# GpSimd's instructions in a hand-scheduled attention and convolution kernel: with and without semaphore ties to VectorE's planned instructions

## The chip, the core and the metric

The kernel runs on one core of a Trainium2 chip. The core has five engines with an instruction stream each: TensorE (PE in the profile; PEld is its weight load), ScalarE (ACT), VectorE (DVE), GpSimd (POOL) and SyncE (SP), which issues most of the DMAs. They meet only through semaphores. The metric is the device time of one execution in microseconds, lower is better.

## What is computed

From `q`, `k`, `v` and `x` (2048 positions, width 640) the kernel computes a gated sum of two branches:

```python
g = sigmoid((A_q * gate_w).sum(-1, keepdims=True))
a = A_q * (causal_long_convolution(kv, ssm_k) + kv * ssm_D)   # kv = short_convolution(A_k, 4 taps) * A_v
b = attention(B_x)   # the reference hands it x = A_q; 32 heads of 20, one shared key and value head
return g * a + (1 - g) * b
```

The attention has 32 heads x 2048 x 2048 scores, and each needs an exponential. The long convolution (over 2048 positions for each of 640 channels) is done through a discrete Fourier transform, written as matrix products with tables of cosines and sines.

## The kernel before

**The streams.** The kernel is a Python program that first collects every instruction as an `Op` (engine, function, operations it depends on, planned cost), then lets a planner, class `Scheduler`, run through planned time and fix the order of each engine's instructions, and then emits each engine's list with semaphore waits. Nothing is decided on the chip: each engine runs its list in order, and an instruction starts when its semaphores are there.

**Attention.** Scores of 128 keys x 512 queries are made by TensorE (line 1323) in PSUM, three or two tiles at a time. ScalarE takes the exponential of 1536 or 1024 columns at a time (line 1360, tiles `ETA` and `ETB`), and TensorE multiplies the result with the values (line 1413). This goes on from about 19 us to the end of the span. A part of the score tiles, named in the table `DVE_J`, has its exponential computed on VectorE: TensorE writes 128 x 512 scores in one of the banks 5 and 7, VectorE brings them to SBUF scaled (line 1393, `dW`, two of them), and three instructions on 128 x 1024 elements make a polynomial of them: lines 1405 and 1406 (`dX`) and 1408 (`ETd`). The last of these feeds TensorE's product again. There are 113 such exponentials. They read both operands from SBUF. Where the program marks an instruction of VectorE `port=True`, the planner takes it that it and a GpSimd instruction can't run at the same time; lines 1405, 1406 and 1408 are marked so, and the evacuations from PSUM are not.

**Normalising.** When a group of four heads is done, VectorE copies its sums (line 1487, `acc`), the reciprocals of the denominators go out to DRAM and come back broadcast (`rbc`), and GpSimd multiplies (line 1499), which for 24 of the 31 groups a DMA of SyncE stores.

**The convolution** fills what the attention leaves free. TensorE transforms the data and the filter (line 1705), VectorE brings the spectra to SBUF (line 1718 `X`, 1724 and 1726 `K`, in three buffers), and GpSimd multiplies them: six instructions per block (line 1738: three products `Pp<-X,K`, one sum `Pp<-Pp`, two `AB<-Pp`), 240 in all. TensorE transforms back from `AB` (line 1773). GpSimd also makes half of the tables (lines 998, 1008, 1010) earlier on. `Pp` has one buffer.

**The planner and GpSimd.** At each step the planner takes the engine whose planned time is least. For GpSimd, once the attention has started (`main_started`), `pool_may` says whether it may start now: not when VectorE is about to begin a marked instruction, yes when VectorE is in an unmarked one that still has some time to go, or when VectorE has nothing marked to do, or when the instruction has waited too long (`WAITP`, 6 us). `place` then fixes the instruction: it works out start and end, appends it to its engine's list, and, in the lines that the change touches, adds a dependency of a GpSimd instruction on a VectorE instruction. I call this a tie. `emit` turns each dependency that isn't covered by an earlier wait into a semaphore wait. The ties come after the start and end are worked out, so that the planner's order doesn't depend on them.

Of the kernel before, what the change touches and what calls it, by code (L numbers as in the profile page):

```python
# [40 lines left out]
HOLD = 0.05  # L41
# [130 lines left out]
class Scheduler:  # L172
# [305 lines left out]
    def place(self, op, e):  # L478
        t = self.t[e]
        op.eng = e  # L480
        if e == "pe":
            mode = MODE.get(op.name, "f")
            if mode != self.mode:
                t += SWITCH
                self.mode = mode
        if op.alts:
            for x in op.alts:
                self.cand[x].discard(op)
            op.fn, op.cost = op.alts[e]
        else:  # L490
            self.cand[e].discard(op)
        if op.main and e == "pe":
            for b in op.banks or ():
                if not self.bank_claimed[b]:
                    self.bank_claimed[b] = True
                    op.deps.update(self.bank_last[b])
        start = max(t, op.ready)
        if e == "pe" and start < COLD:
            op.cost *= 1.85
        if op.kind == "d":  # L500
            if op.nbytes:
                begin = max(start + 0.1, self.dma_bw)
                self.dma_bw = begin + op.nbytes / 300e3
                op.end = max(self.dma_bw, start + op.iss) + op.lat
            else:
                op.end = start + op.iss + op.lat
            self.t[e] = start + op.iss
            best = min(range(NLANES), key=lambda l: self.lanes[l][-1].end if self.lanes[l] else -1.0)
            op.lane = best
            if self.lanes[best]:  # L510
                op.deps.add(self.lanes[best][-1])
            self.lanes[best].append(op)
            op.value = 16 * len(self.lanes[best])
        else:
            if op.port and e == "dve":
                op.end = max(start, self.pool_until - PORTP) + op.cost
                self.port_until = op.end
            elif e == "pool":
                op.end = max(start, self.port_until - PORTD) + op.cost
                self.pool_until = op.end  # L520
            else:
                op.end = start + op.cost
            self.t[e] = op.end
        op.start = start
        op.placed = True
        if e == "pe" and op.cost > 0.05:
            self.active.append((op.end - op.cost * 0.92, op.end))
        if e == "pe":
            if op.name != "qk":
                self.rows = set()  # L530
            elif op.cont:
                self.rows.add(op.row)
            else:
                self.rows = {op.row}
        if op.name in ("tp0", "tp1"):
            b = STAGES[int(op.name[2])][2]
            self.bank_claimed[b] = self.bank_busy[b] = False
            self.bank_last[b] = [op]
            self.bank_ready[b] = op.end + LATX
        if op.name == "pv":  # L540
            if op.stage is not None:
                self.filler = self.filler2[op.stage]
            self.can_fill = not op.last
            self.acc = None
        elif op.name == "acc":
            self.acc = op
        if e == "pool" and self.main_started and HOLD:
            d = self.order["dve"]
            if len(d) > 1 and d[-1].end > t and not d[-1].port:
                op.deps.add(d[-2])  # L550
            elif len(d) > 1 and op.ready + TIED < t:
                op.deps.add(d[-1] if d[-1].end <= t else d[-2])
        self.order[e].append(op)
        self.linear.append(op)
        gr = op.grp
        if gr is not None:
            if e == "pe" and op in gr.mms:
                gr.pos += 1
                if gr.pos == len(gr.mms) and self.open is gr:
                    self.open = None  # L560
            elif op in gr.evacs:
                if all(x.placed for x in gr.evacs):
                    b = gr.bank
                    self.bank_busy[b] = False
                    self.bank_last[b] = [gr.mms[-1]] + list(gr.evacs)
                    self.bank_ready[b] = max(x.end + (LATX if self.main_started else LATS[x.eng, "pe"]) for x in gr.evacs)
        for s in op.succ:
            s.nun -= 1
            lat = 0.0 if (s.eng == "pe" and e == "pe") else self.lat_of(op, e, s.eng)
            s.ready = max(s.ready, op.end + lat)  # L570
            sg = s.grp
            if sg is not None and s.eng == "pe" and not (op.grp is sg):
                sg.nun -= 1
                sg.ready = max(sg.ready, op.end + lat)
                if sg.nun == 0:
                    self.gcand.add(sg)
            if s.nun == 0:
                self.enable(s)
# [91 lines left out]
PORTD = 0.14  # L670
PORTW = 0.2
COVER = 0.3
TIED = 0.1
COLD = 5.6
BUBBLE = 0.04
INB = ()
# [1242 lines left out]
```

## Time and profile before

| what | value |
|---|---|
| time, median of 3 runs | 856.3 us (855.84 to 857.56) |
| the profiled execution's own time | 857.9 us |
| its span, first to last instruction | 856.1 us |
| mean granted clock of TensorE | 0.996 |
| GpSimd busy in the span | 403.2 us, 357 instructions |
| VectorE busy in the span | 772.8 us, 984 instructions |
| line 1738, `Pp<-X,K`, 120 instructions: mean of one, idle time before them | 1388 ns, 114.2 us |
| line 1738, `AB<-Pp`, 80 instructions | 828 ns, 81.4 us |
| line 1738, `Pp<-Pp`, 40 instructions | 1343 ns, 55.3 us |
| lines 1405, 1406, 1408, 113 instructions each: mean of one | 1338, 1385, 1390 ns |
| line 1393, 226 instructions: mean of one | 683 ns |

How to read it: "busy" is the time in which an engine had an instruction in progress. "Idle before" is the time in which the engine stood still ahead of an instruction; the profile puts it down to the semaphore that came last, and names the instruction that gave it. An instruction that has started may still be held up inside; then its record is longer, and it counts as busy. A row of the timeline has the start in us from the span's start, the duration, engine, line, operation, tiles and shape, and in brackets the idle time ahead and what ended it.

### The profile page before, as it was taken

What the parts mean: (1) busy time and instruction counts of PE and PEld (TensorE: products, weight loads), DVE (VectorE), ACT (ScalarE), POOL (GpSimd) and SP (SyncE); (2) the same over time, 40 slices, a digit from 0 to 9 for tenths busy, and PEclk for the clock granted to TensorE, in tenths of its full rate; (3) what the DMA queues carried; (4) which work ended last, traced back from release to release, by engine and by line L of the source; (5) the groups of instructions that cost most, each with busy time, mean ns of one, the idle gap of its engine ahead of it and who ended that gap; (6) DMA issues with size and microseconds to landing.
All of it is one profiled execution on the core that took longest, in us unless ns stands there. A gap on an engine that the chain in (4) does not pass through costs nothing.

```text
span 856.1 us, 18905 instructions
## 1 busy us (share of the span) xinstructions
PE 833.9 (97%) x8094; PEld 349.3 (41%) x8105; DVE 772.8 (90%) x984; ACT 838.3 (98%) x750; POOL 403.2 (47%) x357
## 2 busy tenths in 40 slices
PE   9999999999999999999999999999999999999997
PEld 5244433443444434444334444444443443433334
DVE  7788989895998999999999999999988799989996
ACT  7999989999999999999999999999999999999997
POOL 3578403458464365446417664655666645000000
PEclk9999999999999999999999999999999999999999
DMA  6840240002110001000110202001000000411101
GB/s 190 204 113 15 38 82 21 15 13 65 37 43 20 15 20 28 25 21 21 39 47 20 45 20 46 26 10 43 20 20 16 20 8 8 113 38 60 40 31 44
DMA packets 55765, 36.31 MB, mean 42 GB/s; under 512 B 33057, under 2 KB 51714, under 8 KB 55682
## 3 DMA queue, kind: packets, MB, share of 16 engines
q1 hardware_dynamic: 55106, 34.90, 15.3%
q8 instruction: 63, 1.03, 0.5%
q10 hardware_dynamic: 576, 0.22, 0.1%
q14 instruction: 20, 0.16, 0.1%
HBM read 20.31 MB, written 8.51 MB: 34 GB/s over the span
## 4 chain that ended last, share of the span: by engine, by line
ACT 76%; PE 13%; DVE 8%; DMA 1%; issue 1%; SPq 0%
ACT ETA L1360 46%; ACT ETB L1360 31%; PE ps L1323 4%; PE ps L1413 3%; DVE dX L1406 2%; DVE dX L1405 2%; PE ps L1773 2%; DVE ETd L1408 1%; DVE dW L1393 1%; PE ps L1803 1%; PE ps L1705 1%; DMA xn<-in_A_q_dram 1%; PE ps L1859 1%; PE ps L1230 1%; DMA den<-acc 1%
## 5 line engine op out<-in xcount | busy, mean ns | idle before, releaser
L1360 ACT ACTIVATE ETA<-ps 128x1536 bf16<-128x1536 f32 x365 | 568.3, 1557 | 4.0 <-PE ps L1323 3.5
L1360 ACT ACTIVATE ETB<-ps 128x1024 bf16<-128x1024 f32 x364 | 414.0, 1137 | 2.3 <-PE ps L1323 1.3
L1323 PE MATMUL ps<-qT,kT 32*128 32x512 bf16 (+2 forms) x2176 | 300.4, 372 | 10.1 <-ACT ETA L1360 2.7
L1738 POOL TENSOR_TENSOR Pp<-X,K 128x512 f32<-128x512 bf16 x120 | 165.4, 1388 | 114.2 <-DVE ETd L1408 43.9
L1393 DVE TENSOR_SCALAR dW<-ps 128x512 f32<-128x512 f32 x226 | 154.3, 683 | 26.7 <-PE ps L1323 25.7
L1323 PEld LDWEIGHTS ps<-qT,kT 32*128 32x128 bf16 x2176 | 77.4, 91 | 233.0 <-ACT ETB L1360 112.3
L1408 DVE SCALAR_TENSOR_TENSOR ETd<-dX,dW 128x1024 int16<-128x1024 f32 x113 | 157.1, 1390 | 5.2 <-PE ps L1413 4.9
L1406 DVE SCALAR_TENSOR_TENSOR dX<-dX,dW 128x1024 f32<-128x1024 f32 x113 | 156.5, 1385 | 0.8
L1413 PE MATMUL ps<-ETA,vaug 128*32 128x512 bf16 (+2 forms) x1166 | 152.9, 373 | 0.1
L1405 DVE SCALAR_TENSOR_TENSOR dX<-dW 128x1024 f32<-128x1024 uint16 x113 | 151.2, 1338 | 1.9
L1413 PE MATMUL ps<-ETB,vaug 128*32 128x512 bf16 (+2 forms) x774 | 146.6, 374 | 0.8 <-ACT ETA L1360 0.8
L1738 POOL TENSOR_TENSOR AB<-Pp 128x256 bf16<-128x256 f32 x80 | 66.2, 828 | 81.4 <-DVE dX L1405 28.2
L1773 PE MATMUL ps<-AB,Tcs 128*128 128x256 bf16 x600 | 90.8, 276 | 0.3
L1705 PE MATMUL ps<-ssm_kT,Tcs 128*128 128x256 bf16 x600 | 89.3, 275 | 0.3 <-DVE dW L1393 0.2
L1705 PE MATMUL ps<-kv,Tcs 128*128 128x256 bf16 x600 | 88.5, 276 | 0.6 <-DVE dW L1393 0.5
L1738 POOL TENSOR_TENSOR Pp<-Pp 128x512 f32<-128x512 f32 x40 | 53.7, 1343 | 55.3 <-DVE dX L1406 26.7
L1859 PE MATMUL ps<-Tcs,zeros 128*32 128x512 bf16 (+2 forms) x936 | 75.8, 379 | 3.6 <-DVE acc L1487 3.0
L1773 PEld LDWEIGHTS ps<-AB,Tcs 128*128 128x128 bf16 x600 | 51.4, 98 | 37.2 <-issue 29.5
L1499 POOL TENSOR_TENSOR oTn<-acc,rbc 128x512 bf16<-128x512 f32 x24 | 41.9, 1747 | 51.3 <-issue 30.8
L1705 PEld LDWEIGHTS ps<-ssm_kT,Tcs 128*128 128x128 bf16 x600 | 51.0, 98 | 36.6 <-issue 24.9
L1705 PEld LDWEIGHTS ps<-kv,Tcs 128*128 128x128 bf16 x600 | 49.6, 98 | 37.2 <-issue 27.4
L1499 POOL TENSOR_TENSOR oT<-acc,rbc 128x512 bf16<-128x512 f32 x7 | 12.5, 1787 | 105.0 <-DVE outsb L1806 51.8
(148 smaller groups left out, 634.3 us busy)
## 6 DMA issues: line engine op xcount, KB each, us to landing
rbc<-scr_d SPq DMA_DIRECT2D x31, 256.0 KB
scr_o<-oTn SPq DMA_DIRECT2D x24, 128.0 KB
kv<-in_A_v_dram SPq DMA_DIRECT2D x4, 640.0 KB
out_dram<-outsb SPq DMA_DIRECT2D x15, 160.0 KB
xn<-in_A_q_dram SPq DMA_DIRECT2D x3, 640.0 KB
scr_q<-xT SPq DMA_DIRECT2D x15, 128.0 KB
qT<-scr_q SPq DMA_DIRECT2D x12, 160.0 KB
oTp<-scr_o SPq DMA_DIRECT2D x12, 160.0 KB
```

What stands on the lines that cost most here:

```text
L1323: return e.matmul(self.bank(bk, n, n * t), T["kT4"][32 * r:32 * r + 32, 128 * jt:128 * jt + 128], T[k][32 * r:32 * r + 32, g, q0:q0 + n], ...
L1360: op("act", lambda e: e.activation(et(n)[:, 0:w], self.ps[:, lo:lo + w], ACT.Exp, scale=SCALE), [("ps", base[n % 2] + k) for k in range(le ...
L1393: self.evac(gr, "dve", lambda e, bk, c=c: e.tensor_scalar(W[:, c], self.bank(bk), SCALE * LOG2E * 128.0, 128.0 * (127 - KDN) - 32768.0, AL ...
L1405: V(lambda e: e.scalar_tensor_tensor(X[:, :], w, DP, w, ALU.add, ALU.mult), [kW], ["dX"], c_dve(1024), **k)
L1406: V(lambda e: e.scalar_tensor_tensor(X[:, :], X[:, :], DQ, w, ALU.add, ALU.mult), [kW], ["dX"], c_dve(1024), **k)
L1408: V(lambda e: e.scalar_tensor_tensor(E, X[:, :], DA, W[:, :], ALU.mult, ALU.add), [kW, "dX"], [("ETd", pe)], c_dve(1024), **k)
L1413: return op("pe", lambda e: e.matmul(self.bank(b, n)[32 * r:32 * r + 32, :], T[va][:, j, :], src, start=(j == 0), stop=(j == NSC - 1), til ...
L1499: self.pool(lambda e: e.tensor_tensor(out, T["acc"][:, :], T["rbc"][:, :], ALU.mult), ["acc", "rbc"], [key], 1.27, prio=p, port=True, name ...
L1705: self.mm(gr, lambda e, bk, lhs=lhs, rhs=rhs, comp=comp, n=n: e.matmul(self.bank(bk, 256, 256 * comp), lhs, rhs, start=(n == 0), stop=(n = ...
L1738: f = lambda e: e.tensor_tensor(out, a, b, alu)
L1773: self.mm(gr, lambda e, bk, lhs=lhs, fc=fc, comp=comp, h=h: e.matmul(self.bank(bk, 256, 256 * h), lhs, AB[:, fc, :, comp, :], start=(fc == ...
L1859: sch.filler, *sch.filler2 = ([[lambda e, r=r, st=st, b=b, n=n: e.matmul(self.bank(b, n)[32 * r:32 * r + 32, :], self.T["zeros"][:, 0:32], ...
```

## The change

In `Scheduler.place`, the tie is left out, and with it the constant that only it uses:

```diff
@@ Scheduler.place
         elif op.name == "acc":
             self.acc = op
-        if e == "pool" and self.main_started and HOLD:
-            d = self.order["dve"]
-            if len(d) > 1 and d[-1].end > t and not d[-1].port:
-                op.deps.add(d[-2])
-            elif len(d) > 1 and op.ready + TIED < t:
-                op.deps.add(d[-1] if d[-1].end <= t else d[-2])
         self.order[e].append(op)
         self.linear.append(op)
@@
 PORTW = 0.2
 COVER = 0.3
-TIED = 0.1
 COLD = 5.6
```

The first branch tied a GpSimd instruction that the planner starts while VectorE is in an unmarked instruction (`d[-1]`) to the VectorE instruction before that one (`d[-2]`). The second tied one that was ready over 0.1 us earlier than the planner starts it, to the last VectorE instruction that has ended by then. Without them a GpSimd instruction waits for the semaphores of its operands and buffers. The order of every engine's instructions stays the same, and every other dependency stays.

## The prediction

> **What bounds the kernel now.** I read the page's first part, then the chain that ended last, then the waits of ScalarE, VectorE and GpSimd in the stretch from 110 to 740 us, where nearly all of GpSimd's multiply-accumulate runs, then what line 1738 waits for, and last the timeline of VectorE beside that of GpSimd. From the page, engines with busy us and share of the span, and the chain by engine:
>
> ```profile
> PE 833.9 (97%) x8094; PEld 349.3 (41%) x8105; DVE 772.8 (90%) x984; ACT 838.3 (98%) x750; POOL 403.2 (47%) x357
> ...
> ACT 76%; PE 13%; DVE 8%; DMA 1%; issue 1%; SPq 0%
> ```
>
> ScalarE's exponentials set the end; VectorE is on the chain for 8%. What ScalarE still loses between 110 and 740 us is 5.1 us:
>
> ```profile
> ACT ETA L1360 <- PE ps L1323: 2.7, 3, 1.3
> ACT ETB L1360 <- PE ps L1323: 1.3, 1, 1.3
> ACT ETB L1360 <- PE ps L1413: 1.1, 1, 1.1
> ```
>
> So there is about 5 us to win, and much more to lose. What holds line 1738 (GpSimd's 240 multiply-accumulate instructions) back, in us and times:
>
> ```profile
>   DVE dX L1406: 91.8, 45
>   DVE ETd L1408: 72.2, 34
>   DVE dX L1405: 56.8, 37
> ```
>
> No operand of line 1738 comes from those three lines. These 220.8 us in 116 waits are the ties and nothing else; the change takes them all away.
>
> **Why the place matters.** The three instructions of an exponential on VectorE (lines 1405, 1406, 1408; I call them polynomials) and GpSimd's instructions stop each other. From the timeline, GpSimd and then VectorE:
>
> ```profile
> 230.68 1.16 POOL L1738 TENSOR_TENSOR Pp<-X,K 128x512 f32<-128x512 bf16 x1 [1.16 <-DVE dX L1405]
> 233.00 1.27 POOL L1738 TENSOR_TENSOR Pp<-Pp 128x512 f32<-128x512 f32 x1 [1.16 <-DVE dX L1406]
> ```
> ```profile
> 231.13 1.79 DVE L1406 SCALAR_TENSOR_TENSOR dX<-dX,dW 128x1024 f32<-128x1024 f32 x1
> 232.84 0.68 DVE L1718 TENSOR_SCALAR X<-ps 128x512 bf16<-128x512 f32 x1
> 233.44 1.91 DVE L1408 SCALAR_TENSOR_TENSOR ETd<-dX,dW 128x1024 int16<-128x1024 f32 x1
> ```
>
> A polynomial alone takes 1.21 us; here it takes 1.79, because GpSimd's product ran from 230.68 to 231.84 and the polynomial got through only then. The evacuation of line 1718 beside a running GpSimd instruction takes its usual 0.68. So the cheap place for a GpSimd instruction is the gap of evacuations between two polynomials, and the tie puts it there: it waited for line 1406 to end, 1.16 us, and began 0.08 us later. What costs time in the kernel is the part of it that sticks out of the gap. All such excess over 1.21 us, in the 339 polynomials, is 55.3 us.
>
> **The change, in three parts.** I laid the planner's lists of VectorE and GpSimd beside the rows of the trace (both have the same length) and took, for each GpSimd instruction, the end of its predecessor and of its data, and the tie. 330 run after 18 us; 305 have a tie; 173 of these were held by it for over 0.05 us. Part by part, with the rest of the timeline held still:
>
> A. *95 of 173 stay in their place.* Their predecessor ended while the polynomial that they are tied to was running, and an evacuation follows it. Without the tie such an instruction is issued in the polynomial and waits for it all the same. What changes is how soon it begins. 70 GpSimd instructions of this trace were issued into a polynomial; by their end less their usual duration they got through 0.14 us before its recorded end (median). 150 tied ones began 0.08 us after it. So each is 0.22 us earlier, and sticks out less: the excess they cause falls from 21.6 to 10.8 us. **-10.8 us on VectorE.**
>
> The Trainium skill, page "SBUF — State Buffer", section "A bandwidth-pool intuition that's wrong (but worth ruling out)", has the loser of that port blocked until the VectorE instruction's end plus about 115 ns. The 70 rows say 0.14 us before the recorded end, so this trace doesn't agree, and I go by the rows; by the page an A instruction would begin 0.035 us later than with the tie, and A would be a loss of about 3 us instead.
>
> B. *78 of 173 move forward to a worse place.* An example, GpSimd and then VectorE:
>
> ```profile
> 306.95 0.72 POOL L1738 TENSOR_TENSOR AB<-Pp 128x256 bf16<-128x256 f32 x1 [1.16 <-DVE dX L1406]
> 309.27 1.16 POOL L1738 TENSOR_TENSOR Pp<-X,K 128x512 f32<-128x512 bf16 x1 [1.59 <-DVE ETd L1408]
> ```
> ```profile
> 307.97 1.22 DVE L1408 SCALAR_TENSOR_TENSOR ETd<-dX,dW 128x1024 int16<-128x1024 f32 x1
> 309.11 0.68 DVE L1718 TENSOR_SCALAR X<-ps 128x512 bf16<-128x512 f32 x1
> 309.71 0.68 DVE L1393 TENSOR_SCALAR dW<-ps 128x512 f32<-128x512 f32 x1
> ```
>
> The product at 309.27 fits two evacuations and delays nobody. Its data were there (K at 304.07), its predecessor ended at 307.68; without the tie it starts at 307.7, before the polynomial at 307.97, and ends at 308.86, which holds that polynomial up for 0.84 us. Counted so for all 78 (it starts at once, or 0.14 us before the end of the polynomial in progress; the next polynomial gets through 0.05 us before its end; in the 88 rows where one waited it was 0.13, so the counts are a little high, the old ones too), their excess goes from 16.9 to 48.0 us. 54 delays are over 0.5 us, 0.81 on average. **+31.1 us on VectorE.** Thirteen of the 78 are line 1499's, whose broadcast DMA I didn't date; they are 3.6 us of it.
>
> C. *Slipping in.* Of 122 instructions that wait behind a polynomial, 25 came free less than 0.22 us after it began. For 10 of them the predecessor is an A, now 0.22 us earlier: they get in front. 10 x 0.8 less 10 x 0.2 of old excess: **+6 us**.
>
> Sum on VectorE: -10.8 + 31.1 + 6 = **+26 us**. Bounds: A alone, -11; all 173 as dear as B's (48.0/78 = 0.62 each), 173 x 0.62 - 38.5 = +68.
>
> *What else moves.* GpSimd's results come earlier, and that buys nearly nothing: AB waited at least 3.8 us for TensorE (median 59), line 1499's result left its accumulator free 11 us (median) before VectorE rewrote it. Its store to DRAM on SyncE's queue goes out earlier, and SyncE's later issues are held no longer. VectorE's own waits for GpSimd (line 1718, 5.2 us in 4) mostly go. No new wait holds anything: a data wait that a tie used to cover is for an earlier VectorE instruction. When GpSimd and a waiting polynomial meet, the polynomial goes first (at 312.76 one was waiting, and the GpSimd instruction issued at 312.83 took 2.16 us), so the two alternate and neither starves.
>
> **From VectorE's delay to the end.** VectorE has cover: between 110 and 740 us it waits 39 us for TensorE, but unevenly (1.6 us of idle in 360 to 460). A delay reaches ScalarE through the bank that line 1393 empties: in the rows TensorE reuses it 0.16/0.64/1.08 us later (quartiles), and the next scores are ready 0.14/0.34/0.58 us before their exponential. Together 0.30/0.98/1.66 us of slack. A delay of 0.81 us then costs about 0.6 us in the worst quarter, 0.2 in the next, else nothing: 0.20 on average. 64 such delays (54 and 10) cost 12.8 us; the milder ones that disappear gave 36 x 0.06 = 2.2; A gives back a quarter of 10.8, 2.6. **+8 us.** Bounds: nothing (the waits cover all) and the whole VectorE sum. The profiled execution took 857.9 us (span 856.1 and 1.8 around it), so 865.9 on that scale; on the median shown, 856.3, it is **864.3 us**.
>
> **The rivals.** Differences under 0.2% (1.7 us) are what a measurement of this kernel can't tell from none.
> - *Forecast*, 0.50: 858 to 873.
> - *VectorE becomes the bound*, 0.19: the lags add up, since instructions that run early free the next ones to run early too, and order is fixed on all engines. For: VectorE 90% busy, 99% in 410 to 460. Against: it idles 39 us on TensorE. Price: the 26 us pass nearly whole, or half of the bound of 68: 873 to 890.
> - *All absorbed*, 0.17: For: of the 20 us that A and B add together, some 15 fall in stretches of 50 us in which VectorE idles longer than what they add there. Or GpSimd mostly waits for data instead (against it: the 116 waits). 854.6 to 858.
> - *Faster*, 0.14: one mechanism, A's earlier port, at the gap of one evacuation (0.6 us), where it takes 0.22 us off each overhang. It decides if B costs under some 5 us more than it did. Price: at most ScalarE's 5.1 us of waits, likely 3: 851 to 854.6.
>
> Likeliest: 864.3. The range, 853 to 880, holds the forecast, the absorbed case, some of the faster and half of the saturated case. Faster 0.14, same 0.17, slower 0.69.
>
> **What would show it.** Line 1738's waits on the three polynomial lines gone; its products longer in the record (mean 1388 ns now), as they wait at the port instead; the polynomials' busy sum up from 464.8 by some 26 us; ScalarE's waits for TensorE up from 5.1 towards 13. If the polynomials' sum doesn't grow, B failed; if it grows and ScalarE's waits don't, the step from VectorE to the end did.

## The result and the profile after

The changed kernel takes 880.8 us (879.9 to 884.3), 1.0293 of before (95% interval 1.0267 to 1.0319): 24.5 us more. The forecast was 864.3 us, 8 us more: its sign was right, its size a third of the measured one. Lines behind the change are six or seven up in the changed kernel: 1738 is 1731, the polynomials 1405, 1406 and 1408 are 1398, 1399 and 1401.

From the page of the changed kernel, busy us by engine, and the chain that ended last:

```profile
PE 843.4 (96%) x8105; PEld 350.8 (40%) x8105; DVE 790.0 (90%) x984; ACT 843.4 (96%) x750; POOL 466.3 (53%) x357
...
ACT 39%; PE 31%; DVE 26%; issue 2%; DMA 1%; SPq 0%
```

VectorE's share of the chain went from 8% to 26%, TensorE's from 13% to 31%, ScalarE's from 76% to 39%. But VectorE is busy 90% of the span, as before. What line 1731 waits for now, in us and times:

```profile
  DVE K L1719: 59.8, 11
  DVE AB L1749: 23.5, 5
```

The 220.8 us on the polynomials are gone; what is left are waits for the spectra (`K`) and for the one buffer of `Pp`, which VectorE's line 1749 reads. The polynomials, with busy us and mean ns of one after the bar:

```profile
L1398 DVE SCALAR_TENSOR_TENSOR dX<-dW 128x1024 f32<-128x1024 uint16 x113 | 163.9, 1450 | 1.9
L1399 DVE SCALAR_TENSOR_TENSOR dX<-dX,dW 128x1024 f32<-128x1024 f32 x113 | 164.0, 1452 | 0.8
L1401 DVE SCALAR_TENSOR_TENSOR ETd<-dX,dW 128x1024 int16<-128x1024 f32 x113 | 156.1, 1381 | 4.4 <-PE ps L1406 4.1
```

Their sum is 484.0 us, against 464.8. ScalarE's waits between 110 and 740 us, 5.1 us before, are 25.3:

```profile
ACT ETA L1353 <- PE ps L1316: 19.8, 33, 1.4
ACT ETB L1353 <- PE ps L1316: 4.4, 6, 1.5
ACT ETB L1353 <- PE ps L1406: 1.1, 1, 1.1
```

One such loss, followed from its cause. In the kernel before, the polynomial and the GpSimd instruction of the same place in the lists:

```profile
359.22 1.31 DVE L1408 SCALAR_TENSOR_TENSOR ETd<-dX,dW 128x1024 int16<-128x1024 f32 x1
```
```profile
358.18 1.27 POOL L1738 TENSOR_TENSOR Pp<-Pp 128x512 f32<-128x512 f32 x1 [2.44 <-DVE dX L1406]
360.61 0.73 POOL L1738 TENSOR_TENSOR AB<-Pp 128x256 bf16<-128x256 f32 x1 [1.16 <-DVE ETd L1408]
```

In the changed kernel, VectorE, GpSimd, TensorE and ScalarE in the same stretch:

```profile
370.99 2.32 DVE L1401 SCALAR_TENSOR_TENSOR ETd<-dX,dW 128x1024 int16<-128x1024 f32 x1
373.23 0.68 DVE L1386 TENSOR_SCALAR dW<-ps 128x512 f32<-128x512 f32 x1
```
```profile
368.74 2.13 POOL L1731 TENSOR_TENSOR Pp<-X,K 128x512 f32<-128x512 bf16 x1
370.95 1.27 POOL L1731 TENSOR_TENSOR Pp<-Pp 128x512 f32<-128x512 f32 x1
```
```profile
373.96 0.39 PE L1316 MATMUL ps<-qT,kT 32*128 32x512 bf16 x1 [0.83 <-DVE dW L1386]
```
```profile
375.86 1.45 ACT L1353 ACTIVATE ETA<-ps 128x1536 bf16<-128x1536 f32 x1 [1.12 <-PE ps L1316]
```

`Pp<-Pp` used to sit from 358.18 in the two evacuations ahead of the polynomial at 359.22, which took 1.31. Now its predecessor, issued at 368.74 into a polynomial, ran late in that gap, it follows at 370.95, 0.04 us ahead of the polynomial, and the polynomial takes 2.32. The evacuation behind it ends at 373.91, TensorE waits 0.83 us for its bank and ScalarE 1.12 us for the scores. Lined up exponential by exponential, the changed kernel loses its time in some fifty steps of 0.2 to 1.7 us, nearly all of it between 110 and 740 us of the old span.

### The profile page after: what moved, and what is told of

The parts are those of the page before. It is cut to its first block, busy times and chain, and to the rows that moved or that the text cites. A ratio compares the mean times of both kernels' runs of the same rounds, so it can differ in the third digit from the quotient of the medians.

```text
span 882.5 us, 18755 instructions
## 1 busy us (share of the span) xinstructions
PE 843.4 (96%) x8105; PEld 350.8 (40%) x8105; DVE 790.0 (90%) x984; ACT 843.4 (96%) x750; POOL 466.3 (53%) x357
## 4 chain that ended last, share of the span: by engine, by line
ACT 39%; PE 31%; DVE 26%; issue 2%; DMA 1%; SPq 0%
ACT ETA L1353 24%; ACT ETB L1353 15%; PE ps L1316 10%; PE ps L1698 7%; DVE dX L1399 6%; DVE dX L1398 6%; PE ps L1406 6%; DVE ETd L1401 5%; PE ps L1766 5%; DVE dW L1386 5%; PE ps L1852 2%; DVE acc L1480 1%; DVE X L1711 1%; PE ps L1796 1%; DMA xn<-in_A_q_dram 1%
## 5 line engine op out<-in xcount | busy, mean ns | idle before, releaser
L1353 ACT ACTIVATE ETA<-ps 128x1536 bf16<-128x1536 f32 x365 | 560.2, 1535 | 22.8 <-PE ps L1316 21.7
L1353 ACT ACTIVATE ETB<-ps 128x1024 bf16<-128x1024 f32 x364 | 404.9, 1112 | 5.5 <-PE ps L1316 4.4
L1316 PE MATMUL ps<-qT,kT 32*128 32x512 bf16 (+2 forms) x2176 | 306.2, 373 | 17.2 <-DVE dW L1386 8.0
L1731 POOL TENSOR_TENSOR Pp<-X,K 128x512 f32<-128x512 bf16 x120 | 194.0, 1636 | 84.7 <-DVE K L1719 59.8
L1386 DVE TENSOR_SCALAR dW<-ps 128x512 f32<-128x512 f32 x226 | 154.0, 682 | 36.0 <-PE ps L1316 35.3
L1398 DVE SCALAR_TENSOR_TENSOR dX<-dW 128x1024 f32<-128x1024 uint16 x113 | 163.9, 1450 | 1.9
L1399 DVE SCALAR_TENSOR_TENSOR dX<-dX,dW 128x1024 f32<-128x1024 f32 x113 | 164.0, 1452 | 0.8
L1492 POOL TENSOR_TENSOR oTn<-acc,rbc 128x512 bf16<-128x512 f32 x24 | 37.0, 1541 | 161.5 <-DMA rbc<-scr_d 161.5
L1731 POOL TENSOR_TENSOR AB<-Pp 128x256 bf16<-128x256 f32 x80 | 101.2, 1265 | 4.5
L1731 POOL TENSOR_TENSOR Pp<-Pp 128x512 f32<-128x512 f32 x40 | 72.3, 1807 | 2.4
```

The costliest lines, as they stand in the source:

```text
L1316: return e.matmul(self.bank(bk, n, n * t), T["kT4"][32 * r:32 * r + 32, 128 * jt:128 * jt + 128], T[k][32 * r:32 * r + 32, g, q0:q0 + n], ...
L1353: op("act", lambda e: e.activation(et(n)[:, 0:w], self.ps[:, lo:lo + w], ACT.Exp, scale=SCALE), [("ps", base[n % 2] + k) for k in range(le ...
L1386: self.evac(gr, "dve", lambda e, bk, c=c: e.tensor_scalar(W[:, c], self.bank(bk), SCALE * LOG2E * 128.0, 128.0 * (127 - KDN) - 32768.0, AL ...
L1398: V(lambda e: e.scalar_tensor_tensor(X[:, :], w, DP, w, ALU.add, ALU.mult), [kW], ["dX"], c_dve(1024), **k)
L1399: V(lambda e: e.scalar_tensor_tensor(X[:, :], X[:, :], DQ, w, ALU.add, ALU.mult), [kW], ["dX"], c_dve(1024), **k)
L1492: self.pool(lambda e: e.tensor_tensor(out, T["acc"][:, :], T["rbc"][:, :], ALU.mult), ["acc", "rbc"], [key], 1.27, prio=p, port=True, name ...
```

## The experiments

Theory 1, after the result: a polynomial held up by a whole GpSimd instruction delays VectorE by 0.8 to 1.0 us, and such delays reach the end with little taken off. Rivals: every GpSimd instruction that runs early costs something; the slack of the prediction holds and the time is lost elsewhere (GpSimd's writes, the clock, other waits). Line numbers differ by a few from kernel to kernel; the instructions are the same. A ratio is the time over that of the kernel before in the same session, with its 95% interval in brackets.

**One part alone: the 95, the 78.** The sets A and B of the prediction are written into the kernel as places in GpSimd's list (the list is shortened here):

```diff
-        if e == "pool" and self.main_started and HOLD:
+        if e == "pool" and self.main_started and HOLD and len(self.order["pool"]) not in FREE:
...
+FREE = frozenset((30, 35, 41, ...))   # the 95; the 78 in the other kernel
```

> Ties dropped only for the 95 GpSimd instructions that, in the trace of before, wait for the polynomial in progress and would get the port at its end all the same; the other 210 ties stay. Theory 1 (a whole polynomial's delay, not the tie's latency, makes the loss, and it reaches the end undiminished): the polynomials' sum falls from 464.8 us by up to 10 us, or stays where some slip in front (part C); time 853 to 860 us. Rival (any GpSimd instruction that runs earlier costs, in proportion to how many are freed): 95 of 173 freed, so 13 of the 24.5 us: about 870 us.

> Ties dropped only for the 78 GpSimd instructions that would move forward to a place in front of a polynomial; the other 227 ties stay. Theory 1: this holds nearly all of the loss: the polynomials' sum rises by 15 to 30 us and the time is 870 to 882 us. Rival (in proportion to the freed ones): 11 of the 24.5 us, about 867 us. Rival (the slack of my prediction holds and the loss comes from elsewhere): under 865 us.

The 95 freed: ratio 0.9995 (0.9983 to 1.0007). The polynomials, 455.8 us in all, 9.0 less than before:

```profile
L1409 DVE SCALAR_TENSOR_TENSOR ETd<-dX,dW 128x1024 int16<-128x1024 f32 x113 | 153.1, 1355 | 5.3 <-PE ps L1414 4.9
L1407 DVE SCALAR_TENSOR_TENSOR dX<-dX,dW 128x1024 f32<-128x1024 f32 x113 | 152.7, 1352 | 0.8
L1406 DVE SCALAR_TENSOR_TENSOR dX<-dW 128x1024 f32<-128x1024 uint16 x113 | 150.0, 1328 | 1.9
```

The 78 freed: 872.3 us against 855.7 in the same session, ratio 1.0189 (1.0173 to 1.0206). Polynomials 483.0 us, 18.2 more:

```profile
L1406 DVE SCALAR_TENSOR_TENSOR dX<-dW 128x1024 f32<-128x1024 uint16 x113 | 166.4, 1473 | 1.9
L1407 DVE SCALAR_TENSOR_TENSOR dX<-dX,dW 128x1024 f32<-128x1024 f32 x113 | 160.1, 1417 | 0.8
L1409 DVE SCALAR_TENSOR_TENSOR ETd<-dX,dW 128x1024 int16<-128x1024 f32 x113 | 156.5, 1385 | 5.3 <-PE ps L1414 5.0
```

So it isn't the number of freed instructions: 95 cost nothing, 78 cost 16.6 us. Two thirds of the loss is B, where theory 1 had expected nearly all of it.

**The ties that held nothing.** The same edit with A and B together, with the other 132, and with B and the 132.

> Ties dropped for both sets, the 95 and the 78; the 132 ties that held nothing for more than 0.05 us in the trace of before stay. Freed alone the 95 gave the polynomials -9.0 us and the time nothing, the 78 gave +18.2 us and +16.6 us; with all ties gone it is +19.2 and +24.5 us. Theory 1 (the rest, some +10 us on VectorE and +8 on the time, comes from freeing both together: a GpSimd instruction that runs early lets the next one run early): polynomials' sum 478 to 486 us, 876 to 884 us. Rival (the 132 ties that held nothing in the old order start to hold when GpSimd runs early, so they keep most of the rest): 868 to 873 us, as with the 78 alone.

> Ties dropped only for the 132 GpSimd instructions that their tie held up by no more than 0.05 us in the trace of before; the 173 others keep theirs. Theory 1 (these ties are met when the predecessor and the data are, and matter only once GpSimd runs early): as before, 853 to 858 us, polynomials' sum 460 to 468 us. Rival (they hold places in other executions of before than the profiled one, or by less than 0.05 us at points that decide): 859 to 864 us.

> Ties dropped for the 78 and the 132; the 95 keep theirs. With the 78 alone it was +16.6 us, with the 78 and the 95 +17.9, with all +24.5. Theory 1 (the 132 hold once GpSimd runs early, and about half of every us that a polynomial becomes longer reaches the end): the rest of 6.6 us comes back, 876 to 882 us, the polynomials' increases over before add up to 42 to 50 us. Rival (the rest needs the 95 to be free, since they make GpSimd early): 870 to 874 us.

Ratios: A and B 1.0209 (1.0189 to 1.0228). The 132: 1.0002 (0.9992 to 1.0012). B and the 132: 1.0199 (1.0182 to 1.0216). Against all ties gone, 1.0293, some 7 us are missing in both mixed sets, so neither expectation of theory 1 for a mixed set came true: with A and B, 874.0 us lies below theory 1's 876 to 884 and 1 us above the rival's 868 to 873 (the polynomials' sum, 480.3 us, is in theory 1's 478 to 486); with B and the 132, 873.3 us is what the rival said, and the polynomials grew by 37.9 us where theory 1 had 42 to 50. GpSimd instructions of the 132, which hadn't waited for their ties before, wait for them once A and B are free (busy us, mean ns, idle before and its releasers):

```profile
L1739 POOL TENSOR_TENSOR Pp<-X,K 128x512 f32<-128x512 bf16 x120 | 189.1, 1590 | 126.0 <-DVE K L1727 46.3 <-DVE dW L1394 22.1 <-DVE acc L1488 16.2
```

`dW` and `acc` give line 1739 (1738 of before) no operand: these 38 us are ties that came alive. With B and the 132 freed it is the 95 that are still tied: the same products wait 33.8 us for `ETd` and 18.4 us for the second `dX`. That these waits are what keeps the missing 7 us away is likely, but no run shows it by itself.

**A delay without GpSimd.** All ties stay; VectorE gets 28 instructions more, ahead of 28 polynomials.

```diff
-                for op in self.order[e]:
+                for k, op in enumerate(self.order[e]):
+                    if e == "dve" and k in SLOW:
+                        self.idle(eng, k % 16)
...
+        sch.idle = lambda e, c: e.tensor_reduce(self.T["ksum"][:, c:c + 1], self.T["kT4"][:, 512:1272], AX.X, ALU.max)
```

> All ties stay. 28 dummy instructions of VectorE (a maximum over 760 columns of a constant tile, about 0.85 us, one operand from SBUF) are put ahead of the 28 polynomials that in the changed kernel were held up by over 0.8 us and in the kernel before by under 0.5 us. GpSimd is not part of the delay. Theory 1 (a delay of VectorE reaches the end whole, whatever makes it): 28 x 0.85 = 24 us, so 874 to 884 us. Rival (the slack of my prediction, 0.2 to 0.3 of a delay): 861 to 865 us.

> The 28 dummies of 0.93 us ahead of 28 other polynomials, evenly spread over those between 110 and 740 us that neither kernel held up by 0.3 us. Theory 1 (the schedule has nowhere to put a delay of VectorE): the rows of before give 0.72 us at the worst for all polynomials against 0.63 for the first 28, so +13 to +18 us, 869 to 874 us. Rival (the first 28 are special places): under +8 us.

> As with the 28 dummies of 0.93 us, at the same 28 polynomials, but 340 columns each, about 0.45 us. The first dummies gave +14.6 us, 0.52 us each. By the rows of before, a delay of VectorE of 0.93 us is short by 0.63 us at the worst of the 16 times that TensorE needs something of VectorE before VectorE has idled the delay away, one of 0.45 us by 0.26 us at the worst of 11; at the first time alone 0.47 and 0.17. Theory 1 (the worst of many counts): 28 x 0.26 less the same share lost between TensorE and ScalarE (0.52 of 0.63): about +6 us, 861 to 863 us. Rival (the first time counts, as I had it): under +3 us. Rival (delays pass whole, in proportion): +7 us or more.

The dummies and ScalarE's costliest wait, of the first kernel (28 places taken from the changed kernel):

```profile
L1871 DVE TENSOR_REDUCE ksum<-kT 128x1 f32<-128x760 bf16 x28 | 26.1, 931 | 0.0
```
```profile
ACT ETA L1363 <- PE ps L1326: 10.7, 26, 1.2
```

and of the kernel with 340 columns:

```profile
L1871 DVE TENSOR_REDUCE ksum<-kT 128x1 f32<-128x340 bf16 x28 | 13.8, 493 | 0.0
```
```profile
ACT ETA L1363 <- PE ps L1326: 4.3, 14, 0.7
```

28 x 0.93 us: 1.0170 (1.0153 to 1.0186), +14.6 us, 0.52 each. At 28 other polynomials: 1.0174 (1.0157 to 1.0191), +14.9 us, 0.53 each. 28 x 0.49 us: 1.0053 (1.0038 to 1.0068), +4.5 us, 0.16 each. The first is under what theory 1 said (874 to 884) and over the rival's 861 to 865: a delay doesn't pass whole. The other places behave alike. A straight line through the two sizes: of a delay some 0.3 us is free, and of what exceeds it about 0.8 goes through ((0.52 - 0.16) / (0.93 - 0.49) = 0.82). No third size was run, and the polynomials changed too (8.2, 10.3 and 7.7 us grown, 5.0, 8.6 and 4.5 shrunk, in the order of these three kernels), so the dummies' own cost is somewhat less than these figures. The half-size run lies between theory 1's +6 and the other rival's +3 and so doesn't decide whether the first use or the worst of several uses by TensorE counts.

**GpSimd without reads.** The changed kernel, no ties:

```diff
-            f = lambda e: e.tensor_tensor(out, a, b, alu)
+            f = lambda e: e.memset(out, 0.0)
```

> The changed kernel, without ties, in which line 1738's 240 multiply-accumulate instructions only fill their outputs with zeros, so that they read no operand: the convolution's result is left out. All their waits stay. Theory 1 (the loss is GpSimd's reading that stops polynomials): the polynomials' excess shrinks to what the other GpSimd instructions make, their sum from 484 to 410 to 420 us, and the time is 850 to 856 us although no tie is left. Rival (GpSimd's early phase costs in some other way, by its writes or its waits): the time stays over 865 us.

```profile
L1401 DVE SCALAR_TENSOR_TENSOR ETd<-dX,dW 128x1024 int16<-128x1024 f32 x113 | 142.9, 1265 | 5.8 <-PE ps L1406 5.4
L1398 DVE SCALAR_TENSOR_TENSOR dX<-dW 128x1024 f32<-128x1024 uint16 x113 | 142.8, 1264 | 1.9
L1399 DVE SCALAR_TENSOR_TENSOR dX<-dX,dW 128x1024 f32<-128x1024 f32 x113 | 140.3, 1242 | 0.8
```

1.0011 (0.9998 to 1.0024), polynomials 426.0 us. Without ties, but also without reads, the whole loss is gone: 857.0 us, 1 us over the expected 850 to 856, where the kernel before, run beside it, took 856.0. The sum is 6 us over the expected 410 to 420; the other GpSimd instructions still read. 39 polynomials ran beside fills alone (by over 0.1 us): 1.216 us on average, against 1.213 for 259 that ran beside nothing and 1.571 for 41 beside an instruction that reads. The Trainium skill, page "SBUF — State Buffer", section "Who interferes with whom", says that a VectorE instruction with two SBUF inputs contends with a GpSimd instruction that reads SBUF and not with one that only writes it. These three means agree. (The fills are also shorter, 0.53 us against 1.16, so part of the change in time could be their length; that 39 polynomials beside them weren't held up at all is not.)

**Tied one instruction earlier.**

```diff
-                op.deps.add(d[-2])
+                y = d[-2]
+                op.deps.add(d[d.index(y) - 1] if y.port else y)
...
-                op.deps.add(d[-1] if d[-1].end <= t else d[-2])
+                y = d[-1] if d[-1].end <= t else d[-2]
+                op.deps.add(d[d.index(y) - 1] if y.port else y)
```

> Every tie to a polynomial or another marked instruction of VectorE goes to the VectorE instruction just before it instead, so that the GpSimd instruction is issued while the polynomial runs and waits at the port, not at the semaphore. Theory 1: places stay those of before, each tied GpSimd instruction begins 0.22 us earlier against the polynomial's end; GpSimd's records grow by about 1.1 us each, the polynomials' sum falls from 464.8 us by 5 to 15 us, and the time is 851 to 856 us, since ScalarE has no more than 5 us of waits to win. Rival (a GpSimd instruction issued so early often gets in front of the polynomial): sum up, 862 to 880 us.

```profile
L1408 DVE SCALAR_TENSOR_TENSOR dX<-dX,dW 128x1024 f32<-128x1024 f32 x113 | 151.8, 1344 | 0.8
L1410 DVE SCALAR_TENSOR_TENSOR ETd<-dX,dW 128x1024 int16<-128x1024 f32 x113 | 149.2, 1321 | 5.5 <-PE ps L1415 5.1
L1407 DVE SCALAR_TENSOR_TENSOR dX<-dW 128x1024 f32<-128x1024 uint16 x113 | 146.2, 1294 | 1.9
```

Polynomials 447.2 us, 17.6 less than before, and the time 854.3 us against 855.7: 0.9982 (0.9971 to 0.9992). It is the only version measurably faster than both kernels, by 1.4 us, as theory 1 said and with the gain where it said (the sum fell a little more than the expected 5 to 15). The gain is under the 0.2% that the prediction took for the limit of a measurement; it stands on 12 runs against 21.

**All versions together.** For each, the polynomials' lengths were compared one by one with those of before; the sums of those that grew and those that shrank stand apart.

| version | grew, us | shrank, us | time, us |
|---|---|---|---|
| 95 freed | 6.5 | 15.5 | -0.2 |
| 132 freed | 3.2 | 1.9 | -0.3 |
| tied one earlier | 5.0 | 22.6 | -1.4 |
| no reads, none tied | 11.4 | 50.2 | +0.9 |
| 78 freed | 34.2 | 16.1 | +16.6 |
| 78 and 132 freed | 37.9 | 23.9 | +16.8 |
| 78 and 95 freed | 40.4 | 24.9 | +17.9 |
| all freed (the change) | 47.9 | 28.8 | +24.5 |
| 28 dummies of 0.93 us | 26.1 (dummies) | | +14.6 |

From the fifth row on the time is 0.44 to 0.56 of what grew. Where little grew, in the first four rows, half of it would be 1.6 to 5.7 us, and the time lies 2 to 5 us under that. Either what shrank pays a little (some 0.1 to 0.2 us per us in the three rows where much shrank), or the lengthenings in these rows are small enough to be free; these runs can't tell.

## Why the prediction was wrong

- *What bounds the kernel, and what the ties do*: right. The 220.8 us of waits were ties and vanished, products of line 1738 grew from 1388 to 1636 ns in the record, since they now wait for the polynomial inside the instruction.
- *Part A, -10.8 us on VectorE*: right, measured -9.0 with the 95 alone (6.5 grown, 15.5 shrunk). The 115 ns after the end, which the prediction took from the page "SBUF — State Buffer" and which that page measured on GpSimd's writing of DMA descriptors, would have made it +3; the rows were the better guide.
- *Part B, +31.1 us*: sign right, too large; the 78 alone gave +18.2 net. What shrank, 16.1 us, is close to the 16.9 that the prediction had these instructions cost before; what grew, 34.2, is well under its 48.0. The count held the rest of the timeline still; which part of that made it too high isn't shown.
- *Part C, +6 us*: no run frees it alone. What A and B freed together give beyond each by itself is 15.5 - 18.2 + 9.0 = +6.3 us, and the other 132 ties add 3.7 more; that the ten instructions of C make the 6.3 isn't shown. *Sum* +26, measured +19.
- *From VectorE's delay to the end, +8 us*: **this step failed, by the cost that it gave one delay.** It had 0.20 us lost per delay of 0.81 us; a delay of 0.93 us made on purpose loses 0.52, and by the line through the two dummy sizes one of 0.81 loses 0.42. ScalarE's waits, which were to go from 5.1 towards 13 us, went to 25.3. The step took the slack between VectorE and TensorE and the lead of TensorE over ScalarE as two cushions one behind the other, drawn once for each delay. By the rows of before, a delay of 0.81 us at any polynomial is short by 0.35 us on average at TensorE's first use of a VectorE result behind it, and by 0.61 us at the worst of the 15 uses until VectorE has idled it away; about 0.3 us is what a delay has free, by the two dummy sizes. Which of the two reasons weighs more isn't settled. With 0.42 for its 64 delays the step would have had 27 us instead of 12.8, and the sum 878 us. That would have been near for a partly wrong reason: 41 polynomials grew by over 0.5 us (by 0.80 on average), not 64, and the growths as measured, each taken by the line, make only 18.5 of the 24.5 us.
- *Gains and losses netted*: doubtful as well. The step took A's 2.6 us and 2.2 us for the delays that disappear off the loss. Alone, such gains hardly show: A brought 0.2 us (interval -1.5 to +0.6), 17.6 us less on VectorE were worth 1.4 us, 38.8 us less (no reads) nothing that could be measured. ScalarE had only 5.1 us of waits to win. Whether they set off losses elsewhere in the same run isn't settled (see the table).
- *Rivals*: the time lies in the range of "VectorE becomes the bound", 873 to 890. A part of its mechanism shows, the 6.3 us that A and B make only together; but a delay doesn't pass nearly whole (0.52 of 0.93), and VectorE is busy 90% of the span as before and waits longer for TensorE's scores (line 1393: 25.7 us before, 35.3 after). The two wait for each other in turn, in a fixed order; that VectorE's idle time is poor cover because it lies where TensorE is late too is my reading of this. The faster rival's step, A's earlier start, exists; alone it gained nothing measurable.
- *What is left open*: the last 7 us, which come only when no tie at all is left. 8 to 10 us more of grown polynomials than in the two mixed sets, at 0.5, make 4 to 5; a lower clock, below, 2 to 3. That adds up, but it is argued, not shown.

## What to carry to other kernels

An engine that is 90% busy beside one that sets the end isn't 10% free: in a fixed order shared by engines, look how much a single instruction of it can be late (here some 0.3 us), count every lengthening at what it exceeds that, and don't set shortenings against it in full (alone they paid less than 0.1 us per us net here). Where two engines stop each other, a wait that keeps the shorter one out of the way can cost next to nothing (here at most the 1.4 us of the version tied one earlier); its removal is judged by where the instruction will then start, one by one, not by the idle time that goes. Of 305 such ties, 78 carried two thirds of the worth, and in both mixed sets the ties that were left still held GpSimd back.

## What the runs showed of the hardware

**GpSimd gets through before the polynomial's end is on record.** The engines of this kernel don't meet through semaphores alone: a polynomial and a GpSimd instruction that reads SBUF stop each other, at what the prediction calls the port, and no wait in the profile shows it. 70 GpSimd instructions of the trace before, issued into a running polynomial, got through 0.14 us before its recorded end (their own end less their usual duration), where a semaphore starts one 0.08 us after it. Issuing into the polynomial on purpose shortened VectorE's polynomials by 17.6 us.

**TensorE's clock fell to half for 3.41 us at a time after TensorE had stood still.** In the profile before there are two such stretches, at 115.6 and 726.5 us; in the one after there is one of 6.83 us at 114.5 and three of 3.41 us, at 288.5, 725.4 and 752.7 us. Of the changed kernel, by stretches (length, busy us of PE, PEld, DVE, ACT and POOL, then the granted clock):

```profile
286.00:288.00 2.00, 1.22 (x12) 0.42 (x12) 2.00 (x4) 1.67 (x2) 0.70 (x1) 1.00 0.00 0
288.00:290.00 2.00, 2.00 (x14) 0.72 (x13) 1.97 (x3) 1.44 (x2) 0.00 (x0) 0.63 0.00 0
290.00:292.00 2.00, 2.00 (x12) 1.16 (x10) 0.96 (x3) 0.96 (x2) 0.00 (x0) 0.51 0.00 0
292.00:294.00 2.00, 2.00 (x23) 0.97 (x20) 1.70 (x3) 1.64 (x2) 0.00 (x0) 1.00 0.00 0
487.20:490.60 3.40, 2.01 (x20) 0.72 (x18) 3.01 (x5) 2.61 (x4) 1.99 (x2) 1.00 0.03 2
```

TensorE stood still for 0.8 us of the first stretch; in the next 4 us at about half clock ScalarE loses 1.6 us. Standing still doesn't always do it: in the last stretch shown TensorE was idle for 1.4 us, and the clock stayed full. In 21 runs of the kernel before in one session, those with a mean clock of 1.000 took 854.3 us (3), of 0.998 855.3 (9), of 0.995 to 0.996 856.7 (9). A mean of 0.998 is one stretch of 3.41 us at half clock, 0.996 two, so the time goes with about 0.3 us for each us at half clock; that the clock is the cause of it is argued. The changed kernel's three runs have 0.990, 0.992 and 0.994, so in the median one, at 14 us, there are 7 to 10 us more at half clock than in a run of before: some 2 to 3 of the 24.5 us. So a stall of TensorE may cost more than itself.
